# Even output residues from stored states: B at the even steps kept and topped up by accumulating DMAs on GpSimd's queue, in place of K0 and a decayed B

## The chip, the cores and the metric

The kernel runs on one core of one Trainium2 chip. The metric is the device time of one execution in microseconds (us). Five engines work side by side, each on its own instruction queue in order: TensorE (PE, matrix products into PSUM), VectorE (DVE), ScalarE (ACT), GpSimd (POOL) and SyncE (SP, which here only issues DMAs). They meet at semaphores.

## The reference

One input x (2048 steps of 512 channels) goes through two branches, and a gate mixes them.

```python
def _A_ref(x, Lambda_re, Lambda_im, B_re, B_im, C_re, C_im, log_dt, Dskip):
    Lam_bar = jnp.exp(dt * Lam)                     # 512 complex decays
    B_bar = ((Lam_bar - 1.0) / Lam)[:, None] * Bmat
    Bu = jnp.einsum("bld,pd->blp", x + 0j, B_bar)
    for t in range(L):
        h = Lam_bar[None, :] * h + Bu[:, t, :]
        hs.append(h)
    y = 2.0 * jnp.einsum("blp,dp->bld", hseq, Cmat).real + x * Dskip[None, None, :]
...
def _B_ref(x, wqkv, w_phi, wo):                     # 32 heads of 16: linear attention
    phi_q = concat[softmax(pq), softmax(-pq)]; phi_k = the same of pk
    o = phi_q (phi_k^T v) / (phi_q . sum phi_k + 1e-6)
    return o.reshape(B, S, D) @ wo
...
g = _sigmoid((x * gate_w).sum(-1, keepdims=True))
return g * a + (1 - g) * b
```

## The kernel before

The time axis is cut by residue: step t = 8c + r belongs to cell c (256 of them) and residue r (0 to 7), so x lies in SBUF as xT with the 16 tiles ordered by residue (tile ti = 2r + a holds residue r and cells of half a). The 512 complex states are four blocks j of 128 (PT = 4). The factor (Lam_bar - 1)/Lam is folded into C, so that states are driven by plain B.

Branch A, per block j:

- `st_l(j)` scales B by Lam_bar (two scalings of 128x1024 and two VectorE adds) and transposes the result by DMA into LBT: a B that is one step decayed.
- `st_g(j, dst, ri)` forms the drive of two residues at once on PE: four products with BT at residues 1 and 5 (dst 0) or 3 and 7 (dst 1), four with LBT at the even residues just before them, then for dst 1 products with diagonal matrices `dg` (powers of Lam_bar) that carry the drive on to residue 7. The results are copied from PSUM to `uv`.
- `st_z(j)` scans over the 256 cells on VectorE and gives the state at residue 7, in H3; `st_h4(j)` adds residue 3 to H3, and `st_h(j)` makes residues 1 and 5 in H1. So only the odd residues have states.
- `st_c(j)` makes C2, which is C times the folded factor: two scalings of 128x1024 and two VectorE adds. `st_r(j)` makes a second one, WKV[:, 0:2], which is C2 times Lam_bar, for the even residues (their state is the decayed odd state before them). `st_K(dtile)` makes K0T = B times C2 plus the skip on the diagonal, 8 products of 128x512 and one of 128x128 and a copy, four times: the direct effect of the input of an even step on its own output.
- `st_y(n)` (n = 0 to 15, tiles in the order of residues 7, 3, 5, 1, 0, 4, 2, 6) forms the output of a tile: eight products with the states; then four with x: 128x128 ones with the diagonal Dd at odd residues, 128x512 ones with K0T at even residues.

Branch B: `st_k`, `st_v`, `st_q` are the projections (matrix products and copies to SBUF), `feat_max`, `feat_min`, `feat_exp`, `feat_sum` the two softmaxes, `st_a` gathers phi_k^T v. `feat_sum` ends with a DMA transpose of the features of q (phT). `st_o(n)` forms a tile of attention, `st_O` transposes it by DMA (oT), `st_t(n)` adds its product with Wo onto the PSUM bank of `st_y(n)` and scales it by the gate, `st_R` stores it.

The order of everything is written out by hand: ORDER is a list of steps, each token running its step (a Python generator) up to its next `yield`. Each engine takes its instructions in that order. `@` gives the step its PSUM banks, and `:D` puts a copy or a scaling on VectorE in place of ScalarE. GpSimd makes the table of decays near the start (`st_M`) and then has nothing to do. SP issues every DMA but five small ones.

Of the kernel before, what the change touches and what calls it, by code (L numbers as in the profile page):

```python
# [20 lines left out]
P = 128  # L21
# [3 lines left out]
Z@0 Z Z Z Z Z Z B B B B Lk W00@1 W01@2 W00:D W01:D Lk W10@3 W10 W11@4 W11:D Lx T0@1 T0 f1@5 f0@2 f1:D Lx Lx f0 Z f2@6  # L25
V@7 V f2:D f3@4 P T3@0 T1@1 T2@5 f3 k0@2 T3 P P P2 P2 k0 U P2 P2 Lx Lx Lx U P2 Ln U k3@4 P4 U Lv T1 P4 k0 P4 P3 P2 Ln
i1 i3 V2@1 i1 k1@0 k1 k5@2 k1 P3 M V2 Lq i3 i1 gw i1 i1 i3 i3 x0 i3 k4@3 n0 T2 x0 i0 Lq k11@0 k10@6 k5 x0 n0 k3 i0 i2
k10 x0 Lb k4 n0 k2@5 Lb k2 i2 i0 i0 i0 i2 i2 i2 v1@4 k7@6 k7 v1 n0 x0 n0 l0:D L k11 x1 n1 k9@5 k6@1 l1:D l1:D Lx x1
v0@6 n1 x1 n1 l0:D x1 n1 w3@4 l0 l0 l1 l1 l0 x1 n1 l3:D e0 k6 k9 e0 v2@7 v2 v0 x2 n2 s0 w0@3 D w0 x2 v5@0 v5 e1 s0 x2
k8@2 g000@1 n2 x2 l1 k8 s0 n2 s0 s0 g001@5 g001 g001 n2 g000 g000 w2@0 e1 D x2 n2 k13@3 Lx g011@2 s0 l2 k13 x3 s1 s0  # L30
l3 w1@5 w1 Lb s1 Lc g011 g010@1 Lb l3 Lc g011 g011 g010 g010 g010 x3 s1 c0 g100@3 g010 g011 a0@56 x3 g010 g011 a0 z0
e2 x3 z0 n3 s1 k15@7 n3 g111@2 c0 z0 z0 z0 z0 k15 c1:D g101@1 g100 g101 l2 w3 n3 k14@7 z0 c1 g100 g101 l2 c0 k12@4 w2
n3 z0 x3 c1 n3 k14 s1 g110@3 g110 k12 l2 x4 z0 e2 e2 l2 z0 n4 x4 g110 g110 g111 g111 g111 v6@4 h0 H0 l3 x4 g111 g110
g201@7 v4@0 c0 g110 g111 v3@1 n4 H0 z1 z1 q1@2 x4 H0 s1 s1 v6 g200@4 h0 g200 e2 H0 H0 z1 z1 q1 v3 n4 e3 e3 e3 a1 a1 s2
q0@1 q0 z1 s2 z1 q3@2 q3 n4 s2 z1 z1 g200 v4 s2 z1 x4 n4 s2 z1 e3 q2@3 s3 q2 N0 s3 g201 g201 X0 q4@2 q4 s3 X0 h0 h0
g211@4 N0 H1 X0 s2 g211 g211 v7@7 Lc g211 q6@2 q6 e4 q5@3 H1 H1 X0 g210@0 g210 l3 g210 q5 v10@1 v7 g210 e4 g211 g211
s2 s2 g210 g210 s3 N0 s3 h0 h1 z2 z2 v10 s3 N0 Lc h0 a2 a2 z2 e4 z2 a2 a2 e4 c1 H1 X0 N0 H1 q10@4 q7@7 q7 N1 q10 h0 X1
q8@1 q8 g300@0 N1 X1 g301@3 g301 s4 c2 z2 E0 g300 E0 N1 g311@1 g300 s4 z2 g301 s4 X1 E0 g310@4 z2 g311 N1 h1 g311 E0
z2 v11@0 v11 g311 s3 g310 g310 q12@7 g310 g311 c3 X1 g310 s4 s4 z2 g310 z2 v8@0 S0 g311 v14@3 z3 z3 H2 s4 H2 v8 h1 S0
v14 H2 S0 q15@4 z3 v12@1 v12 z3 S0 S0 q12 a3 q11@0 z3 z3 q15 v9@3 v13@1 S0 S0 q13@4 v9 q9@7 q11 z3 H2 H2 v15@0 z3 s3  # L40
a3 h1 h1 h2 s4 s4 a3 a3 a4 q14@3 v13 a4 h1 h1 q9 v15 c3 c3 z3 z3 c3 c2 h2 c2 c2 Lo S0 h2 H3 h2 h2 a4 a4 G H3 H3 h2 G
h2 G H3 H3 y2@7 S0 S0 h3 q14 y1@0 h3 X1 N1 h3 h3 K3@1 G K3 N2 X2 Y Y Y K2@2 K2 y2 Y y1 y1 q13 E1 E1 E1 y2 h3 S0 X2 h3
E1 N2 K0@1 K0 h3 END o0@4 o0 o0 o2@2 S1 o2 K1@6 o0 o2 y7@1 y7 o2 K1 o3@4 r1 S1 o3 N2 S1 X2 N2 o1@2 o1 S1 o1 o1 y3@6 o3
O0 o3 O1 r1 y3 y3 X2 S1 y7 S1 y5@2 y5 y6@3 X2 S1 N2 r0 S1 r0 r0 S1 S1 y0@4 y0 t1 E2 E2 N3 r0 S1 r1 E2 y0 E2 t2 t2 X3
t3 t3 t0 r1 r2:D r2:D t0 S2 y6 X3 R1 t1 o4@6 o4 r2 N3 S2 o5@4 X3 o4 N3 o5 o5 X3 y6 y5 o4 y4@0 y4 o5 y4 o6@6 S2 r3 r3
r2 S2 o6 o6 r3 y9@4 r3 y11@5 y9 y11 S2 S2 o6 S2 o7@6 O2 R0 o7 o7 t4 S2 t5 N3 X3 N3 t4 o7 S2 E3 S2 E3 y9 E3 y11 y14@0
O3 o8@6 t5:D y13@2 o8 o8 y14 S2 t6 o8 E3 S3 R2 o9@6 S3 S3 S3 t7 t6 o9 o9 o9 y8@3 y8 t7 o10@6 S3 S3 S3 S3 y13 o10 y13
y12@1 o10 o10 O4 S3 o11@6 o11 o11 o11 y8 t8 S3 t9 t8:D t9:D S3 y12 o12@6 o12 y12 O5 o12 o12 y10@4 o13@6 o13 o13 o13 R4
y10 y10 O6 o14@6 o14 o14 o14 O7 y14 t10 t10:D o15@6 o15 t11 R3 o15 o15 O8 t11:D y15@34 R5 t12 t13 t12 t13:D R6 t14
t14:D R7 y15 y15 t15 t15:D t15 t15:D R8 R8  # L50
# [16 lines left out]
def kernel(  # L67
# [32 lines left out]
    ZP = 2  # L100
# [63 lines left out]
    K0T = const.tile([P, KT, D], BF16, name="K0T")  # L164
# [14 lines left out]
    dg = pBC.tile([P, 6, PT, P], BF16, name="dg")  # L179
    DG_NMI, DG_MR, DG_MI, DG_NNI, DG_NR, DG_NI = range(6)  # L180
    (S_LR, S_LI, S_NMI, S_MR, S_MI, S_NNI, S_NR, S_NI, S_NBI, S_BR) = range(10)
    par = pBC.tile([P, 21, PT], F32, name="ssm_par")
    dgs = pBC.tile([P, 10, PT], F32, name="dgs")
    dgv = pBC.tile([P, 6, PT, 4], BF16, name="dgv")
    Bn = pBC.tile([P, PT, 2, D], BF16, name="Bn")
    CT = pBC.tile([P, PT, 2, D], BF16, name="CT")
    ft_g = tc.tile_pool(name="feat", bufs=1, reuse_waits="tile")
# [7 lines left out]
    LBT = pAC.tile([P, 2, KT, Pst], BF16, name="LBT")  # L195
# [175 lines left out]
    def st_M():  # L371
# [16 lines left out]
        mn3 = dgs[:, S_NMI:S_NMI + 6, :].rearrange("p (a b) j -> p b a j", b=3)  # L388
# [6 lines left out]
    def st_D():  # L395
        nc.vector.tensor_copy(out=dgv[:].rearrange("p k j f -> p (k j) f"),
                              in_=dgs[:, S_NMI:S_NMI + 6].rearrange("p k j -> p (k j)").unsqueeze(2).to_broadcast([P, 6 * PT, 4]))
        yield
        VT(out=dg[:].rearrange("p k j (c f) -> p (k j) c f", f=4),
           in0=ident[:].rearrange("p (c f) -> p c f", f=4).unsqueeze(1).to_broadcast([P, 6 * PT, 32, 4]),  # L400
           in1=dgv[:].rearrange("p k j f -> p (k j) f").unsqueeze(2).to_broadcast([P, 6 * PT, 32, 4]), op=ALU.mult)
        yield
# [6 lines left out]

    def st_l(j):  # L410
        lr, li = uv[j][:, 0], uv[j][:, 1]
        scaled(lr, Bn[:, j], dgs[:, S_LR, j:j + 1])
        yield
        scaled(li, Bn[:, j], dgs[:, S_LI, j:j + 1])
        yield
        VT(out=lr[:, 0], in0=lr[:, 0], in1=li[:, 1], op=ALU.subtract)
        yield
        VT(out=lr[:, 1], in0=lr[:, 1], in1=li[:, 0], op=ALU.add)
        yield
        trans(out=LBT[:, :, :, j * P:(j + 1) * P].rearrange("p r k s -> p (r k) s"), in_=lr.rearrange("p r d -> p (r d)"))  # L420
        yield
# [156 lines left out]

    def st_g(j, dst, ri):
# [4 lines left out]
        def cells(kt, r):  # L584
            return xT[:, kt, :].rearrange("p (r c) -> p r c", r=8)[:, r::4, :]

# [4 lines left out]
        for kt in range(KT):  # L591
            MM(out=pgq[:], lhsT=LBT[:, ri, kt, js], rhs=cells(kt, r1 - 1), start=False, stop=(dst == 0 and kt == KT - 1))  # L592
# [16 lines left out]

    def st_c(j):  # L610
        t = (Wo, K0T)[j % 2]
        a_, b_ = t[:, 0:2, :], t[:, 2:4, :]
        scaled(a_, CT[:, j], dgs[:, S_BR, j:j + 1])
        yield
        scaled(b_, CT[:, j], dgs[:, S_NBI, j:j + 1])
        yield
        VT(out=C2[:, 0, j], in0=a_[:, 0], in1=b_[:, 1], op=ALU.add)
        yield
        VT(out=C2[:, 1, j], in0=b_[:, 0], in1=a_[:, 1], op=ALU.subtract)
        yield  # L620

    def st_r(j):
        a_, b_ = CT[:, 2 * j % 4], CT[:, (2 * j + 1) % 4]
        scaled(a_, C2[:, :, j], dgs[:, S_LR, j:j + 1])
        yield
        scaled(b_, C2[:, :, j], dgs[:, S_LI, j:j + 1])
        yield
        VT(out=WKV[:, 0, j], in0=a_[:, 0], in1=b_[:, 1], op=ALU.add)
        yield
        VT(out=WKV[:, 1, j], in0=a_[:, 1], in1=b_[:, 0], op=ALU.subtract)  # L630
        yield
# [85 lines left out]
    def st_K(dtile):  # L717
        pk0 = bank([P, D], F32, "pk0")
        ds_ = slice(dtile * P, (dtile + 1) * P)
        for j in range(PT):  # L720
            MM(out=pk0[:], lhsT=Bn[:, j, 0, ds_], rhs=C2[:, 0, j], start=(j == 0), stop=False)  # L721
            MM(out=pk0[:], lhsT=Bn[:, j, 1, ds_], rhs=C2[:, 1, j], start=False, stop=False)  # L722
        MM(out=pk0[:, ds_], lhsT=ident[:], rhs=Dd[:, dtile, :], start=False, stop=True)
        yield
        evac(K0T[:, dtile, :], pk0[:])
        yield
# [14 lines left out]
    def st_y(n):  # L741
# [5 lines left out]
        src = H3 if r % 4 in (0, 3) else H1  # L747
        off = {7: ZP, 0: ZP - 1, 3: ZP + NC, 4: ZP + NC, 1: 0, 2: 0, 5: NC, 6: NC}[r] + a * P
        cw = WKV if r % 2 == 0 else C2
        for j in range(PT):  # L750
            for ri in range(2):
                for py, (c, w) in zip(pys, halves):
                    MM(out=py[:], lhsT=src[:, j, ri, off:off + P], rhs=cw[:, ri, j, c:c + w], start=(j == 0 and ri == 0), stop=False)  # L753
            if j % 2:
                yield
        for kt in range(KT):
            xs = xT[:, kt, ti * P:(ti + 1) * P]
            if r % 2 == 0:
                for py, (c, w) in zip(pys, halves):
                    MM(out=py[:], lhsT=xs, rhs=K0T[:, kt, c:c + w], start=False, stop=False)  # L760
            else:
                MM(out=pys[0][:, kt * P:(kt + 1) * P], lhsT=xs, rhs=Dd[:, kt, :], start=False, stop=False)
# [122 lines left out]
```

## Time and profile before

| | |
|---|---|
| median of 3 runs | 158.71 us (158.57 to 159.26) |
| the profiled execution, its own time | 159.32 us |
| span of that execution, first to last instruction | 157.6 us |
| granted TensorE clock | 1.000 |
| PE busy | 150.5 us, 95% of the span, 1054 matmuls |
| DVE busy | 137.0 us, 87% |
| ACT busy | 126.4 us, 80% |
| POOL busy | 9.3 us, 6% |

The span is shorter than the execution's own time by 1.72 us that lie around it, and the median of the runs is 0.61 us under the profiled execution. "Busy" is the time in which an instruction of the engine was in flight; matmuls overlap each other, so the time that one keeps PE from the next is read from the starts of a run of them, not from its duration. In the lists of groups, the duration of one instruction stands after the busy time, and after the bar the idle time of the engine in front of the group.

### The profile page before, as it was taken

The page shows a single profiled execution, that of the slowest core. Times are in us where ns is not written, and L with a number is a line of the kernel's source. Part 1 is how long each engine was busy: PE and PEld are TensorE (multiplying, and loading weights), DVE is VectorE, ACT ScalarE, POOL GpSimd, SP SyncE. Part 2 cuts the span into 40 slices and gives each one's busy share as a digit, 9 for nine tenths or more (in the row PEclk, how much of TensorE's full clock was granted, in tenths as well). Part 3 has the DMA queues.
Part 4 walks back from the last instruction along what each step waited for, and adds up shares of the span by engine and source line. Part 5 has one row for each costly group of instructions (what it writes and reads, how often), then busy time and mean ns, then how long its engine had stood idle before and what let it go on. Part 6 is the DMA issues. An engine that isn't in the chain of part 4 may idle for free.

```text
span 157.6 us, 2913 instructions
## 1 busy us (share of the span) xinstructions
PE 150.5 (95%) x1054; PEld 77.5 (49%) x1054; DVE 137.0 (87%) x330; ACT 126.4 (80%) x233; POOL 9.3 (6%) x29
## 2 busy tenths in 40 slices
PE   6799799999999999999999999999999999999991
PEld 2554343545444544654444654555455444545570
DVE  4799699999999999999999999989999959553732
ACT  3499899799999999999999999997998496212110
POOL 6007800000000000000000000000000000000000
PEclk9999999999999999999999999999999999999999
DMA  5999989970029200000000019602793996795761
GB/s 133 175 213 280 241 176 205 202 119 4 0 45 178 44 0 6 0 0 0 4 0 0 0 19 264 121 2 49 138 213 95 148 212 154 136 208 128 165 201 33
DMA packets 52407, 16.99 MB, mean 108 GB/s; under 512 B 47145, under 2 KB 52393, under 8 KB 52393
## 3 DMA queue, kind: packets, MB, share of 16 engines
q1 hardware_dynamic: 51776, 16.78, 52.1%
q8 instruction: 8, 0.13, 0.4%
q10 hardware_dynamic: 552, 0.02, 0.2%
q14 instruction: 7, 0.05, 0.1%
q0 software_dynamic: 64, 0.00, 0.0%
HBM read 3.17 MB, written 2.10 MB: 33 GB/s over the span
## 4 chain that ended last, share of the span: by engine, by line
PE 58%; ACT 23%; DMA 8%; SPq 5%; DVE 3%; issue 1%; DVEq 0%
PE PS L753 18%; PE PS L466 9%; PE PS L808 9%; ACT EE L527 6%; PE PS L760 4%; SPq L216 4%; DMA Bn<-in_A_B_im_dram 4%; PE PS L592 3%; ACT Xq L125 3%; ACT uv L125 3%; PE PS L773 3%; PE PS L722 2%; PE PS L721 2%; PE PS L589 2%; DMA LBT<-uv 2%; PE PS L571 2%
## 5 line engine op out<-in xcount | busy, mean ns | idle before, releaser
L527 ACT ACTIVATE EE<-EE 128x1024 bf16<-128x1024 bf16 x32 | 34.6, 1179 | 0.0
L466 PE MATMUL PS<-WKV,xT 128*128 128x512 bf16 x128 | 30.4, 379 | 0.8 <-DMA WKV<-in_B_wqkv_dram 0.8
L466 PEld LDWEIGHTS <-xT 128*128 128x128 bf16 x192 | 18.1, 98 | 21.2 <-DMA WKV<-in_B_wqkv_dram 1.3
L125 ACT CAST Xq<-PS 128x512 bf16<-128x512 f32 x32 | 20.7, 708 | 0.7 <-PE PS L466 0.5
L753 PEld LDWEIGHTS <-H 128*128 128x128 bf16 x136 | 12.8, 98 | 12.9
L786 DVE TENSOR_TENSOR on<-PS,rd 128x512 bf16<-128x512 f32 x16 | 10.7, 687 | 6.9 <-ACT rd L780 6.9
L592 PE MATMUL PS<-xT,LBT 128*128 128x512 bf16 x64 | 15.9, 379 | 0.1
L589 PE MATMUL PS<-xT,BT 128*128 128x512 bf16 x64 | 15.8, 379 | 0.0
L753 PE MATMUL PS<-WKV,H 128*128 128x512 bf16 (+1 forms) x72 | 15.6, 355 | 0.0
L808 PE MATMUL PS<-Wo,oT 128*128 128x512 bf16 (+1 forms) x68 | 15.4, 366 | 0.0
L466 PE MATMUL PS<-Wq,xT 128*128 128x512 bf16 x64 | 15.4, 379 | 0.0
L753 PE MATMUL PS<-C,H 128*128 128x512 bf16 x64 | 14.9, 379 | 0.0
L777 ACT ACTIVATE ld<-PS 128x32 f32<-128x32 f32 x16 | 3.4, 214 | 11.7 <-PE PS L773 11.6
L125 ACT CAST vx<-PS 128x512 bf16<-128x512 f32 x16 | 11.9, 775 | 0.0
L125 ACT CAST uv<-PS 128x256 bf16<-128x256 f32 (+1 forms) x24 | 11.4, 573 | 0.0
L504 DVE TENSOR_TENSOR sm<-EE 128x2048 bf16<-128x2048 bf16 (+1 forms) x9 | 9.9, 1100 | 0.8 <-ACT EE L527 0.8
L592 PEld LDWEIGHTS <-LBT 128*128 128x128 bf16 x64 | 6.1, 98 | 7.7 <-DMA LBT<-uv 0.6
L589 PEld LDWEIGHTS <-BT 128*128 128x128 bf16 x64 | 6.3, 98 | 7.3 <-DMA xT<-in_A_x_dram 0.2
L521 DVE TENSOR_TENSOR EE<-mn,Xq 128x2048 bf16<-128x2048 bf16 (+1 forms) x9 | 9.9, 1097 | 0.0
L515 DVE TENSOR_TENSOR EE<-Xq,mx 128x2048 bf16<-128x2048 bf16 (+1 forms) x9 | 9.9, 1097 | 0.0
L814 DVE TENSOR_SCALAR ot<-PS,G 128x512 bf16<-128x512 f32 (+1 forms) x9 | 6.2, 690 | 4.1 <-PE PS L808 3.9
L542 DVE TENSOR_TENSOR EE<-EE,rc 128x2048 bf16<-128x2048 bf16 x8 | 9.6, 1217 | 0.0
(169 smaller groups left out, 289.7 us busy)
## 6 DMA issues: line engine op xcount, KB each, us to landing
out_dram<-ot SPq DMA_DIRECT2D x7, 256.0 KB, 2.3
C<-in_B_wqkv_dram SPq DMA_DIRECT2D x2, 256.0 KB, 3.1
C<-in_A_x_dram SPq DMA_DIRECT2D x2, 256.0 KB, 5.0
Bn<-in_A_B_re_dram SPq DMA_DIRECT2D x1, 512.0 KB
WKV<-in_B_wqkv_dram SPq DMA_DIRECT2D x1, 512.0 KB
Bn<-in_A_B_im_dram SPq DMA_DIRECT2D x1, 512.0 KB, 6.4
Wo<-in_B_wo_dram SPq DMA_DIRECT2D x1, 512.0 KB
oT<-on SPq DMA_TRANSPOSE x9, 3.2
```

The lines of the kernel that those rows point to most:

```text
L125: nc.scalar.copy(out=out_ap, in_=in_ap)
L466: MM(out=pt[:], lhsT=xT[:, kt, ti * P:(ti + 1) * P], rhs=W[:, kt, :], start=(kt == 0), stop=(kt == KT - 1))
L504: VT(out=dst, in0=cur[:, :, :, 0:n, :], in1=cur[:, :, :, n:2 * n, :], op=op)
L515: VT(out=half(EE, 0), in0=X5, in1=live["mx", p].to_broadcast([P, L, 8, Dh, 4]), op=ALU.subtract)
L521: VT(out=half(live["EE", p], 1), in0=live["mn", p].to_broadcast([P, L, 8, Dh, 4]), in1=X5, op=ALU.subtract)
L527: aexp(out=EE[:, l_], in_=EE[:, l_], func=ACT.Exp)
L542: VT(out=E5[:, u:u + 2], in0=E5[:, u:u + 2], in1=rc[:, u:u + 2].to_broadcast([P, 2, 2 * NB, Dh, 4]), op=ALU.mult)
L589: MM(out=pgq[:], lhsT=BT[:, ri, kt, js], rhs=cells(kt, r1), start=(kt == 0), stop=False)
L592: MM(out=pgq[:], lhsT=LBT[:, ri, kt, js], rhs=cells(kt, r1 - 1), start=False, stop=(dst == 0 and kt == KT - 1))
L753: MM(out=py[:], lhsT=src[:, j, ri, off:off + P], rhs=cw[:, ri, j, c:c + w], start=(j == 0 and ri == 0), stop=False)
L786: VT(out=live["on", g_][:, u], in0=pn[:, :, :, 0:Dh], in1=rd[:].unsqueeze(3).to_broadcast([P, 2, 16, Dh]), op=ALU.mult)
L808: MM(out=py[:], lhsT=oT[:, g, :], rhs=Wo[:, g, h * w:(h + 1) * w], start=False, stop=(g == HG - 1))
```

## The change

Three things change, and ORDER is new.

1. The even residues get states of their own. `st_b(j, pr, ri)` (new) forms B x at two even residues (pr 0: residues 0 and 4, pr 1: 2 and 6), four products of 128x512 and a copy to `eb`. `st_g` takes the decayed drive from `eb` by two products with new diagonals of Lam_bar (dg grows from 6 to 9 of them), where it had four with LBT; `st_l` and LBT go. `st_p(j, pr)` (new) then adds Lam_bar times the odd state before it to `eb`: it scales the states into the buffers t1 and t2, and two DMAs on GpSimd's queue add these to `eb` in place.
2. `st_c` scales into C2 directly, and a DMA on GpSimd's queue adds the second term; its two VectorE adds go.
3. With states at all residues, `st_y` uses C2 throughout and Dd at every residue. `st_r`, `st_K` and K0T go.

`eb` lies in the place of K0T and, for the blocks 2 and 3, in that of Bn. t1 is CT[:, j], and t2 lies in dg. The core of the diff:

```diff
 ORDER = """
-Z@0 Z Z Z Z Z Z B B B B Lk W00@1 W01@2 W00:D W01:D Lk W10@3 W10 W11@4 W11:D Lx T0@1 T0 f1@5 f0@2 f1:D Lx Lx f0 Z f2@6
...
+Z@0 Z Z Lk Lk B Z Z Z Z W00@1 Lx Lx B W01@2 B B W01:D W10@3 T0@4 W11@5 W00:D T1@6 f1@2 T0:D Lv W10 Lx T2@1 V@3 T1:D V
...
+S2 S2 N3 y5@2 p21 y5 S1 y5 o6@0 N3 o7@6 p31:D R0 y4@3 y4 y4 p01 O2 t4 S2 o7 o6 X3 t5 o7 p01 N3 p31:D o6 o6 y9@0 o7 p11
+S2 p21 y9 S2 E3 E3 R1 E3 E3 t4:D O3 o8@6 S2 t5:D y9 y8@1 o8 y8 S3 S3 S3 t6 p21 o8 o8 p01 o9@2 o9 o9 S3 o9 t7 O4 S3
+y11@6 S3 S3 S3 y8 y10@7 t6 t7 o10@2 y10 o10 o10 o11@4 S3 S3 y11 y11 y10 t8 t9 p31 o10 o11 o11 o11 t8:D S3 t9 y14@4
...
+    eb = [eb01[:, 0], eb01[:, 1], Bn[:, 0:2], Bn[:, 2:4]]
...
-        VT(out=dg[:].rearrange("p k j (c f) -> p (k j) c f", f=4),
...
+        for k in range(3):
+            VT(out=dg[:, 3 * k:3 * k + 3].rearrange("p k j (c f) -> p (k j) c f", f=4),
...
-    def st_l(j):
...
+    def st_b(j, pr, ri):
+        pb = bank([P, N2], F32, "pb")
+        for kt in range(KT):
+            MM(out=pb[:], lhsT=BT[:, ri, kt, j * P:(j + 1) * P], rhs=cells(kt, 2 * pr), start=(kt == 0), stop=(kt == KT - 1))
+        yield
+        evac(eb[j][:, ri, pr, :], pb[:])
+        yield
...
-        for kt in range(KT):
-            MM(out=pgq[:], lhsT=LBT[:, ri, kt, js], rhs=cells(kt, r1 - 1), start=False, stop=(dst == 0 and kt == KT - 1))
+        da, db = ((DG_LR, DG_NLI), (DG_LI, DG_LR))[ri]
+        MM(out=pgq[:], lhsT=dg[:, da, j, :], rhs=eb[j][:, 0, dst], start=False, stop=False)
+        MM(out=pgq[:], lhsT=dg[:, db, j, :], rhs=eb[j][:, 1, dst], start=False, stop=(dst == 0))
...
+    def add_by_dma(out_ap, in_ap):
+        nc.gpsimd.dma_start(out=out_ap, in_=in_ap, accum_op=ALU.add)
...
     def st_c(j):
...
+        scaled(C2[:, 1, j], CT[:, j, 0], dgs[:, S_BR, j:j + 1])
+        yield
+        scaled(C2[:, 0, j], CT[:, j, 1], dgs[:, S_NBR, j:j + 1])
+        yield
+        scaled(CT[:, j], CT[:, j], dgs[:, S_NBI, j:j + 1])
+        yield
+        add_by_dma(C2[:, :, j], CT[:, j])
         yield
...
-    def st_K(dtile):
...
+    def st_p(j, pr):
+        E_ = eb[j][:, :, pr]
+        t1 = CT[:, j]
+        t2 = dg[:].rearrange("p k j s -> p (k j s)")[:, 2 * N2 * j:2 * N2 * (j + 1)].rearrange("p (a c) -> p a c", a=2)
+        cuts = ((0, NC, H3, ZP - 1), (NC, N2, H3, ZP + NC)) if pr == 0 else ((0, N2, H1, 0),)
+        for c0, c1, src, z0 in cuts:
+            scaled(t1[:, :, c0:c1], src[:, j, :, z0:z0 + c1 - c0], dgs[:, S_LR, j:j + 1])
+            yield
+        add_by_dma(E_, t1)
+        yield
+        for ri in range(2):
+            for c0, c1, src, z0 in cuts:
+                scaled(t2[:, ri, c0:c1], src[:, j, 1 - ri, z0:z0 + c1 - c0], dgs[:, (S_NLI, S_LI)[ri], j:j + 1])
+                yield
+        add_by_dma(E_, t2)
         yield
...
-        cw = WKV if r % 2 == 0 else C2
+        if r % 2:
+            src = H3 if r % 4 == 3 else H1
+            off = {7: ZP, 3: ZP + NC, 1: 0, 5: NC}[r] + a * P
+            hs = [[src[:, j, ri, off:off + P] for ri in range(2)] for j in range(PT)]
+        else:
+            off = r // 4 * NC + a * P
+            hs = [[eb[j][:, ri, r % 4 // 2, off:off + P] for ri in range(2)] for j in range(PT)]
...
-            if r % 2 == 0:
-                for py, (c, w) in zip(pys, halves):
-                    MM(out=py[:], lhsT=xs, rhs=K0T[:, kt, c:c + w], start=False, stop=False)
-            else:
-                MM(out=pys[0][:, kt * P:(kt + 1) * P], lhsT=xs, rhs=Dd[:, kt, :], start=False, stop=False)
+            h, c = (0, kt * P) if len(pys) == 1 else (kt // 2, kt % 2 * P)
+            MM(out=pys[h][:, c:c + P], lhsT=xs, rhs=Dd[:, kt, :], start=False, stop=False)
```

The names pXY that the prediction uses are ORDER's: p21 is `st_p(2, 1)`, block 2 and residues 2 and 6.

## The prediction

> **What bounds the kernel now.** I read the page's busy tenths first, then the chain of waits, then the windows by stage, and last the groups by shape.
>
> ```profile
> PE   6799799999999999999999999999999999999991
> ACT  3499899799999999999999999997998496212110
> DMA  5999989970029200000000019602793996795761
> PE 58%; ACT 23%; DMA 8%; SPq 5%; DVE 3%; issue 1%; DVEq 0%
> ```
>
> PE is full from slice 8 to slice 39; ACT is nearly as full up to slice 32, then has room. The stages say the same (columns: length, then busy time of PE, PEld, DVE, ACT, POOL, clock, DMA share, GB/s):
>
> ```profile
> 60.00:92.00 32.00, 31.81 (x270) 16.85 (x269) 31.97 (x71) 32.00 (x59) 0.00 (x0) 1.00 0.01 2
> 92.00:120.00 28.00, 28.00 (x207) 14.67 (x205) 27.49 (x62) 27.08 (x49) 0.00 (x0) 1.00 0.58 123
> 120.00:140.00 20.00, 19.97 (x138) 9.93 (x136) 15.47 (x27) 11.02 (x24) 0.00 (x0) 1.00 0.81 154
> ```
>
> Three engines are full at once from 60 to 92 us, GpSimd does nothing there, and the DMA engines rest until 92. Which of the three sets the pace is told by adding up issue intervals. The chain of waits shows PE's (start, length, what):
>
> ```profile
> 99.39 0.45 PE PS L762 x8
> 126.12 1.73 PE PS L760 x8
> 152.35 0.87 PE PS L760 x8
> 153.70 0.92 DVE ot L814 x2
> ```
>
> Eight 128x512 products in 1.73 us are 0.216 each, eight 128x256 in 0.87 are 0.109, eight 128x128 in 0.45 are 0.056. With 0.032 for 128x68 (L773) and 0.025 for one column, the kernel's products are 584 x 0.216 + 48 x 0.109 + 100 x 0.056 + 256 x 0.032 + 64 x 0.025 = 146.9 us. The time at which PE reaches a product, less the product work ahead of it, is 4.2 us at 8 us, 5.6 at 24, 6.3 at 48, 6.7 from 72 to 96, 7.0 at the end. So PE lost its time before 24 us and then 1.4 us in 130: it sets the end, and 3.9 us of scaling and storing follow its last product (153.7 to 157.6). ACT's instructions add up to 123.2 us plus a table load of 1.3, DVE's to 134.4.
>
> **What PE gains.** All of it is on the path, if the others keep up. K0T's forming goes (L721, L722: 32 products of 512 columns and 4 of 128): -32 x 0.216 - 4 x 0.056 = -7.1 us. At even residues Dd takes the place of K0T: 28 of 512 and 8 of 256 go, 32 of 128 come: -6.0 - 0.9 + 1.8 = -5.1. The drive of the even step by `eb` and the new diagonals adds 32 of 512: +6.9. `st_b`'s 64 products take the place of LBT's 64: 0. Net **-5.4 us** (rounded once; 141.5 left).
>
> **ACT** goes up. Gone: 16 scalings of 1024 columns at 1.05, 4 K0T copies at 0.47, 11 scalings of 512 moved to DVE at 0.61, 3 xT copies at 0.48: 26.8 us. New: 5 scalings of 1024 for C2 at 1.05, 14 of 512 at 0.61, 12 of 256 at 0.40 (between the 0.26 of a copy of that size and the 0.61 of 512), 16 copies of `eb` at 0.47, 3 outputs at 0.59, 3 casts at 0.47: 29.3. Net +2.5, giving 125.8. Token by token along the new ORDER, ACT's sum runs at most 0.8 us ahead of PE's (1.2 in the old one), because what is added falls where PE has `st_b`: I put it at 0. If that fails, up to 2.5 is the price.
>
> **DVE** goes down: 24 adds of 512 at 0.335, 8 scalings of 1024 at 0.395, 3 outputs at 0.75, 2 WKV casts at 0.64 and one Xq at 0.33 (15.1 us) go. Three dg instructions for one (+0.9), 3 xT copies (1.0), 3 scalings of 1024 (1.2), 21 of 512 at 0.23 and 4 of 256 at 0.15 (both estimates from the 1024 row, 5.4) come: 8.5. Net -6.6. DVE isn't the bound, so 0.
>
> **The start.** Two things move. The LBT transposes leave SP (`LBT<-uv`, 3.37 us in the chain at 23.06): PE is late for them by about 0.3 only. But the second Wq transpose (H) moves behind two BT and one CT:
>
> ```profile
> 12.45 5.69 SPq L231 DMA_TRANSPOSE H<-in_B_wqkv_dram  x2
> 18.36 3.27 SPq L226 DMA_TRANSPOSE BT<-Bn  x2
> ```
>
> BT can't start before Bn_im lands at 17 to 18.4; then 3.27 for BT, 1.33 for CT and 2.85 for H end the issue at 24.5 to 25.8, and it lands 1.5 to 3 later, at 26 to 28.8. PE wants it at product work 20.2, about 25.8 us: there stands w3, the first piece of the folding of Wq (`fold`), which reads all of it. So 0 to 3 us of stall, and every product queued behind w3 waits with it: I take **+1.0**, from the early half, since a BT for one block of the two needs only part of the 3.27. A gain of 0.8 is possible on the other side: PE's wait for WKV at 16 us (0.84) goes because Wv (Lv) is now needed later.
>
> **The adding DMAs.** Twenty of them (4 for C2, 16 for `eb`), 256 KB each in 256 runs of 1 KB, all through GpSimd's queue. Nothing like them is in the trace. Nearest rows:
>
> ```profile
> L255 POOL DMA_DIRECT2D vec_m<-in_A_Dskip_dram x1 | 0.8, 766 | 0.0
> out_dram<-ot SPq DMA_DIRECT2D x7, 256.0 KB, 2.3
> oT<-on SPq DMA_TRANSPOSE x9, 3.2
> phT<-EE SPq DMA_TRANSPOSE x8, 4.5
> ```
>
> GpSimd's own issue took 0.77 us for 1 KB; a plain 256 KB store lands in 2.3 us, a transpose of the same size in 3.2, of 512 KB in 4.5. An addition reads two operands and writes one, so I take 3 to 4 us from issue to landing (bounds 2.3 and 4.5), and 1.0 us of issue (bounds 0.5, SP's issue of such a store, and 2.85, half of the row of H above, the longest issue of one transpose). Bandwidth is there: a store occupies all 16 DMA engines for about 0.75 us, and 0.01 of the DMA time is used from 60 to 92 us.
>
> What matters is when the sums must be there. In the new ORDER the first even tile (y9) starts at product work 115, about 122.5 us; it reads blocks 2 and 3 of residues 0 and 4 (`eb` in Bn). y14 comes at 134.5 us, y12, which wants p21 and p31, at about 137. The first addition (p01) can be issued at about 84 us, the last (the second of p31) at about 124; p20's second at about 109, 13 us ahead of y9. At 3 to 4 us each, side by side, every sum is early and the cost is 0.
>
> The other cost is in the engines' own order. The two additions to one `eb` are ordered, and t1 and t2 are reused: p10's t1 waits until c1 has landed, p21's until p20's first, p31's until p30's first, p21's t2 until p20's second. ACT waits in its own order: behind such a wait stand branch B's ld, rd and the exponentials, for which `st_o` and so PE wait. By product work the tightest is p31's t1, 1 to 2 us after p30's landing at 3.5 us each; p21's has 4. With landings 1 us longer, ACT waits 0 to 1 us, and it is already near PE. I take **+0.8** for this together with GpSimd's and DVE's meetings (next part); bounds 0 and 4.
>
> **A row and a rule on GpSimd beside DVE.** While DVE ran two 128x1024 instructions between 15.77 and 17.05 us, a GpSimd instruction on 128x16 took far longer than one of the same shape before it:
>
> ```profile
> 13.31 0.21 POOL L375 TENSOR_TENSOR ssm_par<-dgs 128x16 f32<-128x16 f32 x1
> 15.88 1.24 POOL L382 TENSOR_TENSOR ssm_par<-dgs,vec 128x16 f32<-128x16 f32 x1
> 15.77 0.68 DVE L515 TENSOR_TENSOR EE<-Xq,mx 128x1024 bf16<-128x1024 bf16 x1
> 16.37 0.68 DVE L521 TENSOR_TENSOR EE<-mn,Xq 128x1024 bf16<-128x1024 bf16 x1
> ```
>
> GpSimd gave way for the length of what DVE had running: 1.24 against 0.21, ending when DVE did. An issue of 1.0 us may thus become 2, which still leaves 2.7 us on average between additions (85 to 125 us, 15 of them) unfilled. The Trainium skill ("SBUF — State Buffer", section "Who interferes with whom") goes further and speaks against this change: the descriptors of a DMA on GpSimd's queue are written through a port pair that it shares with DVE, one holds it for the whole of an instruction, and the other stands still; two-input VectorE instructions block only GpSimd's reads. The row fits the last part; no run so far shows an issue held. By the skill's "DMA: Bandwidth & Descriptors" (section "Anatomy of one DMA — SWDGE (gpsimd) path") such a transfer takes 2.0 us plus bytes at 436 GB/s, an estimate of 2.6 us for 256 KB, with which my 0.8 would be about 0.3.
>
> **Sum.** 157.6 - 5.4 + 1.0 + 0.8 = 154.0 us of span; plus 1.72 around it 155.7 for a profiled execution; less 0.61 for the median: **155.1 us**. The measurement can tell about 0.5% from no change, so "the same" is 157.9 to 159.5.
>
> **Rivals.**
>
> *R1, the queue works one addition after another, slower.* If an addition holds the queue from its issue to its landing, T each, the fifteen from p01's first (85 us) to p31's last end at 85 + 15T. y12 wants that by 137: up to T = 3.5 us nothing happens. At T = 4.0 they end at 145 and PE stands still 8 us: 155.1 + 8 = 163. At 4.5 it is 15 more: 170. For it: 3.2 to 4.5 us for transposes of such sizes, and the fixed order of adds on one tile. Against: plain stores of 256 KB land in 2.3, and SP's transposes overlap. 0.18.
>
> *R2, DVE is held by GpSimd's issues.* About 19 scalings of DVE fall between p01 and p31. If an issue of 1.0 us shuts out DVE, an issue is under way 16 x 1.0 / 45 = 36% of that time, a DVE instruction waits half an issue on average: 19 x 0.36 x 0.5 = 3.4 us; at 1.5 us, 7.6. DVE is 98% busy at 92 to 120 us, and PE waits for its copies: 158 to 162, 160 the middle. The row above shows the opposite direction only. The shut-out for a whole instruction is also the rule of the Trainium skill's "SBUF — State Buffer" named above, and as yet no row bears it out in this direction. 0.10.
>
> *R3, the start costs more.* H lands at 28.8, 3.0 after w3's turn, and PE has nothing else in its order: 2.0 more than I took, and 0.4 for Wq's copies trailing on ACT: 157.5. 0.10.
>
> *R4, ACT is the bound.* Its +2.5 us falls where ACT is 100% busy (60 to 92), PE's gain is used up by waits for copies, and the end stays about 158.7. Against it: after 120 us ACT is only 55% busy. 0.04.
>
> **How the numbers follow.** Forecast 0.58 (154 to 156.5). R1, R2 above: nearly all slower, with some of R2 in "the same". R3 mostly faster, R4 the same. Faster: 0.58 less 0.03 for costs that take the gain, plus 0.06 of R3 = 0.61. Same: 0.03 + 0.04 of R3 + 0.04 of R4 + 0.02 of R2 = 0.13. Slower: 0.18 of R1 + 0.08 of R2 = 0.26. The range: the low end has no stall at the start, the gain of 0.8 there, and about a third of the 0.8 for landings and meetings unspent (155.1 - 1.0 - 0.8 - 0.3 = 153.0); at the top it takes in R3, R4, R2 and the first of R1, **153.0 to 163.0**, leaving out R1's long half (0.1) and about 0.07 below or between.
>
> **What will show it.** Right: PE's product work near 141.5 us, its lag still about 7 to 8 at y9, no idle PE before y9 and y12; additions landing in 3 to 4 us; GpSimd's issues about 1 us. The first wrong sign for R1: additions landing at equal steps of over 3.5 us, and PE's wait before y9, y14 or y12 ended by a DMA to `eb`. For R2: DVE scalings of 512 columns well above 0.3 us where they lie beside an issue. For R3: a PE wait at w3 ended by the DMA into H. The forecast is wrong if the median is over 157.9.

## The result, and the profile after

The changed kernel takes 168.06 us (median of 4 runs, 165.26 to 168.69) against 158.99 of the kernel before in the same job. The ratio, here and below taken over the undisturbed runs of both alone (here 165.26 and 167.5), is 1.0463 (95% interval 1.0327 to 1.0598): slower, where 155.1 us was forecast. The profiled execution is the one of 165.26 us, its span 163.6. It is the fastest of the four; what the others lose beyond it, 2.2 to 3.4 us, no trace shows.

The page of the kernel after: busy tenths in 40 slices of 4.1 us, DMA queues, and the shares of the chain.

```profile
PE   6899879999999999999999999999389977699990
PEclk9999999999999999999999999999957999999998
DMA  5999999974000004290009999799997699999251
q0 software_dynamic: 5504, 5.25, 24.5%
DVE 27%; ACT 26%; PE 20%; DMA 15%; SPq 7%; issue 2%; DVEq 0%; ACTq 0%
```

PE is full up to slice 27 as before, then has holes (a 3 in slice 28, 7 and 6 in 32 to 34), and for two slices the granted clock falls (5 and 7). The DMA row, which had zeros from slice 14 to 22 and gaps after that, is full from slice 21 on. In the chain PE's share fell from 58% to 20%, DMA's rose from 8% to 15%. Queue 0 is GpSimd's: its twenty additions held 24.5% of the time of 16 engines, 24.5% x 163.6 / 20 = 2.0 us of all sixteen for each (the times of its packets added up; where packets of several transfers are under way at once, each has its own time counted).

Windows of the kernel after (length, busy PE, PEld, DVE, ACT, POOL, clock, DMA share, GB/s; a share over 1: packets of several transfers under way at once):

```profile
60.00:92.00 32.00, 31.54 (x198) 15.43 (x200) 31.99 (x79) 32.00 (x63) 8.57 (x8) 1.00 0.44 60
92.00:120.00 28.00, 24.21 (x217) 13.26 (x219) 27.03 (x64) 25.04 (x52) 10.82 (x9) 0.97 1.18 162
120.00:140.00 20.00, 17.71 (x108) 8.33 (x109) 11.71 (x18) 11.25 (x23) 3.67 (x3) 0.88 1.02 164
```

From 60 to 92 us nothing is wrong. From 92 to 140 us the DMA share went from 0.58 and 0.81 to 1.18 and 1.02, and PE lost time. What it waited for, in the list of waits (engine, line, releaser: total us, times, longest):

```profile
PEld L805 <- DMA oT<-on: 5.2, 2, 2.9
PE PS L805 <- DMA oT<-on: 4.6, 2, 2.8
PE PS L770 <- DMA phT<-EE: 1.8, 2, 1.3
PE PS L457 <- DMA xT<-in_A_x_dram: 1.6, 1, 1.6
```

Not one of them is a sum in `eb`. They are the transposes of branch B, whose own work the change leaves as it was, and an x tile at the start. In the kernel before, the same list has no wait for an oT or a phT. The lists of ScalarE and VectorE after the change have no wait for an addition either. The chain of waits shows the two worst, and the timelines GpSimd's last three additions and SP's issue of the phT behind them (start, length):

```profile
113.71 5.31 DMA oT<-on
119.07 2.74 PE PS L805 x6
130.42 10.63 DMA phT<-EE
141.09 0.43 PE PS L770 x8
```

```profile
128.65 1.20 POOL L611 DMA_DIRECT2D Bn<-dg  x1 [11.22 <-ACT dg L410]
129.38 1.71 POOL L611 DMA_DIRECT2D eb<-dg  x1
130.10 2.21 POOL L611 DMA_DIRECT2D Bn<-dg  x1
130.42 7.82 SPq L549 DMA_TRANSPOSE phT<-EE  x1
```

A phT of 512 KB that landed in 4.5 us before takes 10.63 when three additions are issued just ahead of it: 6.1 us more, and three times 2.0 is 6.0. Most of it is the issue, which holds SP's queue for 7.82 us, against 1.3 to 3.5 for a phT in the kernel before. After the wait for oT, six products take 2.74 us where eight took 1.73: the clock.

PE's arrival less the product work ahead of it (the measure of the prediction) is 6.5 us from 28 to 56 us, 7.7 at 92, 8.1 from 104 to 114; then 11.5 at 119, 14.6 at 126, 16.5 at 136, 18.0 from 141 to the end. 141.5 + 18.0 + 4.1 of tail = 163.6. So the kernel is on the forecast's course up to 114 us (forecast for the end: 8.6) and loses 9.9 us in the next 27.

### The profile page after: what moved, and what is told of

The parts are those of the page before. It is cut to its first block, busy times and chain, and to the rows that moved or that the text cites. A ratio compares the mean times of both kernels' runs of the same rounds, so it can differ in the third digit from the quotient of the medians.

```text
span 163.6 us, 2923 instructions
## 1 busy us (share of the span) xinstructions
PE 148.0 (90%) x1028; PEld 76.5 (47%) x1046; DVE 132.1 (81%) x325; ACT 128.0 (78%) x252; POOL 33.5 (20%) x50
## 3 DMA queue, kind: packets, MB, share of 16 engines
q0 software_dynamic: 5504, 5.25, 24.5%
## 4 chain that ended last, share of the span: by engine, by line
DVE 27%; ACT 26%; PE 20%; DMA 15%; SPq 7%; issue 2%; DVEq 0%; ACTq 0%
ACT EE L518 8%; PE PS L753 7%; DMA phT<-EE 6%; PE PS L805 6%; SPq L218 5%; DMA xT<-in_A_x_dram 4%; PE PS L457 3%; DMA oT<-on 3%; ACT Xq L127 3%; DVE EE L533 3%; DVE sm L495 3%; ACT uv L127 3%; DVE mn L495 2%; DMA Wc<-in_B_w_phi_dram 2%; DVE mx L495 2%
## 5 line engine op out<-in xcount | busy, mean ns | idle before, releaser
L805 PE MATMUL PS<-Wo,oT 128*128 128x512 bf16 (+1 forms) x65 | 16.7, 393 | 4.9 <-DMA oT<-on 4.6
L588 PE MATMUL PS<-xT,BT 128*128 128x512 bf16 x64 | 16.1, 379 | 0.1
L753 PE MATMUL PS<-C,H 128*128 128x512 bf16 x64 | 16.0, 402 | 0.0
L576 PE MATMUL PS<-xT,BT 128*128 128x512 bf16 x64 | 15.6, 379 | 0.1
L809 ACT ACTIVATE ot<-PS,G 128x512 bf16<-128x512 f32 x11 | 7.3, 684 | 10.3 <-PE PS L805 10.3
L127 ACT CAST uv<-PS 128x256 bf16<-128x256 f32 (+1 forms) x24 | 13.1, 633 | 0.0
L611 POOL DMA_DIRECT2D eb<-CT x4 | 4.8, 1324 | 38.0 <-ACT CT L410 37.8
L805 PEld LDWEIGHTS <-oT 128*128 128x128 bf16 x68 | 6.5, 103 | 11.0 <-DMA oT<-on 5.2
L410 ACT ACTIVATE dg<-H,dgs 128x256 bf16<-128x256 bf16 (+1 forms) x18 | 10.8, 675 | 0.0
L127 ACT CAST vx<-PS 128x512 bf16<-128x512 f32 x16 | 10.6, 788 | 0.0
L753 PEld LDWEIGHTS <-H 128*128 128x128 bf16 x64 | 6.5, 104 | 8.1 <-issue 2.2
```

The lines of the kernel that those rows point to most:

```text
L127: nc.scalar.copy(out=out_ap, in_=in_ap)
L410: nc.scalar.mul(out=out_ap, in_=in_ap, mul=s_)
L576: MM(out=pb[:], lhsT=BT[:, ri, kt, j * P:(j + 1) * P], rhs=cells(kt, 2 * pr), start=(kt == 0), stop=(kt == KT - 1))
L588: MM(out=pgq[:], lhsT=BT[:, ri, kt, js], rhs=cells(kt, r1), start=(kt == 0), stop=False)
L753: MM(out=py[:], lhsT=hs[j][ri], rhs=C2[:, 1 - ri, j, c:c + w], start=(j == 0 and ri == 0), stop=False)
L805: MM(out=py[:], lhsT=oT[:, g, :], rhs=Wo[:, g, h * w:(h + 1) * w], start=False, stop=(g == HG - 1))
```

## The experiments

Theory D: the additions fill the DMA engines and delay the transposes on SP's queue. Rival Q: issuing on GpSimd, or waiting for additions, holds VectorE or ScalarE. Rival S: the new order puts the transposes too late by itself. The time of the kernel before beside them was 159.5 to 159.6 us.

### e1: the same DMAs with few bytes

```diff
-        add_by_dma(E_, t1)
+        add_by_dma(E_[:, :, 0:32], t1[:, :, 0:32])
-        add_by_dma(E_, t2)
+        add_by_dma(E_[:, :, 0:32], t2[:, :, 0:32])
```

> The 16 additions to eb carry 64 bytes of each 1 KB run, so 15/16 of what they should add is left out; the number of DMAs, their runs, issues, waits and places in every queue stay. Theory D (the additions fill the DMA engines: 24.5% of 163.6 us for 20 of them is 2.0 us of all 16 engines each, and the transposes oT and phT on SP's queue wait behind them): oT lands in about 3.2 us and phT in about 4.5 again, PE's waits before t2, t6 and o10 go, and with them the half clock after the first: 165 to 168 less about 9 us, 155.5 to 158. Rival Q (issuing on GpSimd, and DVE or ACT held by it or by the waits on the additions): unchanged, 165 to 169. Rival S (the new order puts the transposes too late by itself): unchanged as well.

157.39 us (157.0 to 157.65), 0.9892 of the kernel before (0.9858 to 0.9926). From its page and list of waits:

```profile
PEclk9999999999999999999999999999999999999999
q0 software_dynamic: 5504, 1.31, 9.5%
PE PS L805 <- DMA oT<-on: 1.3, 2, 0.7
```

As many packets as ever (5504), a quarter of the bytes, and 8.3 us gone from the span of the profiled execution (163.6 to 155.3); the two long waits and the drop of the clock with them. Order, issues and queue are those of the kernel after, so S falls, and the issues of Q are worth little. The other half of Q, waiting for additions, is eased here too, since they land sooner (those from CT to `eb` in 2.8 us instead of 5.0); that it isn't the cause rests on the lists of waits above and on e9.

### e2: the six late additions on VectorE

```diff
-        add_by_dma(E_, t2)
+        if (j, pr) in ((2, 0), (3, 0), (1, 1), (2, 1), (0, 1), (3, 1)):
+            VT(out=E_, in0=E_, in1=t2, op=ALU.add)
+        else:
+            add_by_dma(E_, t2)
```

> The six second additions that are issued last (p20, p30, p11, p21, p01, p31) are VectorE adds of 128x1024 at 0.60 us instead of DMAs. Theory D: 12 us of DMA time less after 108 us; PE's waits before t6 and o10 (1.8 + 1.3 us) go and the one before t2 shrinks, since only one or two additions are left near it: 157 to 161. VectorE is full until 112 us, which costs up to 1.2 us. Rivals Q and S: 165 or more.

157.99 us (157.62 to 158.13), 0.9921 (0.9889 to 0.9952): the whole computation, and already faster than the kernel before. Six 0.6 us adds take the place of 12 us of all DMA engines. Five of them run after 118 us, and from 120 to 140 us VectorE is busy for 16.5 of 20 us.

### e6 and e7: which three of the six

```diff
 e6:  if (j, pr) in ((2, 0), (3, 0), (1, 1)):   # issued at 108, 111, 116 us
 e7:  if (j, pr) in ((2, 1), (0, 1), (3, 1)):   # issued at 128.6 to 130.1 us
```

> The changed kernel with the second additions of p20, p30 and p11 (issued at 108, 111 and 116 us) as VectorE adds. Theory D: the wait before t2 (2.8 us) and the half clock after it (about 3 us lost) go, the waits before t6 and o10 (3.3 us) stay: 160 to 163.5. If the half clock doesn't hang on that wait: 163.5 to 166.

> The complement: the second additions of p21, p01 and p31 (issued at 128.6 to 130.1 us) as VectorE adds. Theory D: phT of the last group lands in 4 to 5 us instead of 10.6, the waits before t6 and o10 (3.3 us) go, those before t2 stay with the half clock: 163 to 165.5. Rivals Q and S: 165 to 169 in both of these runs.

162.05 us (159.38 to 162.51; 1.0073, 1.0013 to 1.0133) and 161.13 (159.97 to 162.93; 1.0088, 1.0055 to 1.0121). The first as expected in amount, but the wait that was left took another place; the second below its range. The list of waits of e6, then of e7:

```profile
PE PS L808 <- DMA oT<-on: 4.3, 2, 3.9
```

```profile
PE PS L808 <- DMA oT<-on: 2.2, 1, 2.2
PE PS L773 <- DMA phT<-EE: 0.6, 1, 0.6
```

With PE earlier in e6, the last three additions met an oT (issued at 124.04, landed 7.50 later) instead of the phT, and the clock fell to 0.59 from 132 to 136 us. So each group of three can delay whatever transpose stands behind it; the two losses don't add up to single waits that could be named ahead.

### e3: the additions by GpSimd itself

```diff
-        add_by_dma(E_, t1)
+        nc.gpsimd.tensor_tensor(out=E_, in0=E_, in1=t1, op=ALU.add)
-        add_by_dma(E_, t2)
+        nc.gpsimd.tensor_tensor(out=E_, in0=E_, in1=t2, op=ALU.add)
```

> The 16 additions to eb are GpSimd's own additions of 128x1024 instead of DMAs on its queue. Theory D: nothing of eb passes through the DMA engines, so the transposes land as before, 156 to 158, if GpSimd needs under 2.5 us each (15 of them between 85 and 124 us). Rival Q in the form of a meeting of GpSimd and VectorE: VectorE's instructions beside GpSimd's get longer, and the time stays above 160 although no transpose waits. Rival S: 165 or more.

181.94 us (181.27 to 185.42), 1.1415 (1.1365 to 1.1464). The DMA share from 84 to 124 us is 0.16, and still this is the slowest kernel of all. Rows of its groups and its timeline:

```profile
L715 POOL TENSOR_TENSOR eb<-eb,CT 128x1024 bf16<-128x1024 bf16 x4 | 15.6, 3899 | 40.8 <-ACT CT L410 39.6
91.21 2.21 DVE L412 TENSOR_SCALAR m<-H,dgs 128x512 bf16<-128x512 bf16 x1
99.26 2.61 DVE L681 TENSOR_TENSOR m<-m,uv 128x1024 bf16<-128x1024 bf16 x1
```

In the kernel after these VectorE rows take 0.35 and 0.68 us. VectorE's busy time rose from 132.1 to 159.2 us, and PE's largest waits in total are for VectorE (6.3 and 5.4 us). Beside GpSimd's own additions some VectorE instructions take about as long as an addition (2.4 to 2.5 us there); others keep their time (0.42 for one of 128x512 at 89.73 us), and then it is the additions that are long (two in 9.09 us). That is the meeting that R2 feared, but from GpSimd's arithmetic. Beside its DMA issues, in the kernel after, such a scaling takes what it takes alone (the first row):

```profile
53.64 0.35 DVE L412 TENSOR_SCALAR mc<-H,dgs 128x512 bf16<-128x512 bf16 x1
91.90 1.20 POOL L611 DMA_DIRECT2D Bn<-CT  x1 [4.18 <-DVE m L681]
92.98 0.34 DVE L412 TENSOR_SCALAR mc<-H,dgs 128x512 bf16<-128x512 bf16 x1
93.30 1.20 POOL L611 DMA_DIRECT2D eb<-dg  x1 [0.20 <-issue]
93.51 0.34 DVE L412 TENSOR_SCALAR m<-H,dgs 128x512 bf16<-128x512 bf16 x1
```

Of the six scalings of 512 columns that overlap an issue there, five took 0.34 us and one (at 35.51) 0.50.

### e9, after a flawed e5: the additions alone, on the kernel before

```diff
         aexp(out=rd[:], in_=ld[:], func=ACT.Exp, scale=-1.0, bias=nge[:, ti:ti + 1])
+        for d_ in {0: (dgt[:, 1],), 2: (dgt[:, 2],), 3: (Bn[:, 0],), 4: (Bn[:, 1],), ...}.get(n, ()):
+            nc.gpsimd.tensor_copy(out=after_rd[:], in_=rd[:].rearrange("p a b -> p (a b)"))
+            nc.gpsimd.dma_start(out=d_, in_=dgt[:, 0], accum_op=ALU.add)
```

> The kernel before, with ten adding DMAs of 256 KB on GpSimd's queue between buffers that nothing reads any more (CT, Bn), each released by the rd of a tile of st_o (104 to 130 us). Nothing of its order or work is changed, and no engine waits for them. Theory D (each fills all 16 DMA engines for 2.0 us): the DMA share of 0.58 and 0.81 from 92 to 140 us is 32 us of 48, with 20 more it is over 48, so transposes land 2 to 5 us later and PE waits: 161 to 168. Rival S (the changed order is at fault): 159. Rival Q (issues of 1.2 us hold VectorE): VectorE's instructions beside an issue get longer, ten times up to 1 us, little of it on the path after 120 us: 159 to 161.

> The experiment of ten adding DMAs on the kernel before, mended: there the buffers of CT were still used by st_r, and ScalarE waited 5.9 and 3.5 us for two of the additions. Now nine of them, between dg and Bn, whose last readers have run by 104 us, released by rd of st_o as there. Theory D: 18 us of all 16 DMA engines between 104 and 131 us, beside the 32 that are in use from 92 to 140: phT and oT land later where they meet (up to 6 us for three together), and PE waits for them, 2 to 6 us with any half clock: 161 to 166. Rival S (the changed order alone delays the transposes): 159 to 160.

e5 took 173.85 us (173.01 to 175.16), outside its range, but CT was still read in it, against what its expectation says: a scaling of ScalarE waited 5.9 us for an addition, so it tells little.

e9 has the fault mended: 165.12 us (164.3 to 166.46), 1.0353 (1.0297 to 1.041). From its list of waits and its chain:

```profile
PE PS L813 <- DMA oT<-on: 3.1, 3, 1.5
PE PS L774 <- DMA phT<-EE: 2.3, 1, 2.3
124.71 9.30 DMA phT<-EE
```

(`dgt` is `dg` cut in three.) Old order, old arithmetic, and nine additions that no engine waits for (and nine GpSimd copies of 128x32 that time their issues): 5.6 us lost, at oT and phT again. This is theory D by itself.

### e10: the same DMAs as plain copies

```diff
-        add_by_dma(E_, t1)
+        nc.gpsimd.dma_start(out=E_, in_=t1)
-        add_by_dma(E_, t2)
+        nc.gpsimd.dma_start(out=E_, in_=t2)
```

> The changed kernel with the 16 DMAs to eb as plain copies, same queue, same 256 runs of 1 KB, nothing added (the even states are overwritten instead of summed up). If it is the adding that takes 2.0 us of the 16 DMA engines, and a copy takes the 0.75 of SP's stores, this falls to 156.5 to 159. If it is the queue or its kind of descriptors, whatever they do, it stays at 164 to 169.

158.46 us (156.94 to 162.93), 0.9905 (0.9864 to 0.9945); the even states are overwritten here, not summed up. From its page and its DMA issues, and in the last line from the page of e9:

```profile
q0 software_dynamic: 2432, 5.25, 13.3%
C<-CT POOLq DMA_DIRECT2D x4, 256.0 KB, 4.5
eb<-CT POOLq DMA_DIRECT2D x4, 256.0 KB, 2.8
q0 software_dynamic: 1360, 2.36, 8.6%
```

The bytes are those of the kernel after (5.25 MB). The queue's time is 13.3% of 155.9 = 20.7 us instead of 40.1. In e3, where C2's four are the only additions, queue 0 has 3.8% of 180.4 = 6.9 us, 1.7 for each; less these, a copy costs (20.7 - 6.9) / 16 = 0.87 us, near the store's 0.75. So it isn't the queue. Nor are the packets the same: 64 of queue 0's belong to small loads, so an addition has (5504 - 64) / 20 = 272, and a copy (2432 - 64 - 4 x 272) / 16 = 80. But e9's additions, with (1360 - 64) / 9 = 144 packets each, still held 8.6% x 164.8 / 9 = 1.6 us. Most of the difference is thus put down to the adding; a copy in 272 packets wasn't run.

### e8: PE kept busy in the wait

```diff
+        if n == 5:
+            for _ in range(28):
+                MM(out=pn2[:, 1, 272:512], lhsT=ph[:, 7, :], rhs=Wo[:, 0, 0:240], start=False, stop=True, skip_group_check=True)
```

> The changed kernel with 28 products of 240 columns (2.9 us at 0.103, an estimate from 0.109 for 256) of no use behind st_o(5), into columns of its bank that nothing reads, so that PE is busy while it waits for oT before t2. If the half clock from 118 to 125 us comes from that idle stretch, it goes and the time falls by about 3 us, to 162.5 to 165.5, though PE has more to do; if not, 165 to 169.

164.55 us (162.94 to 165.4), 1.0283 (1.0192 to 1.0374). The profiled execution is 2.4 us shorter than that of the kernel after (161.2 and 163.6), though PE has 2.9 us more to do; the intervals of the two ratios overlap, so the times alone don't tell the kernels apart. The clock does, in the same window of the two, first of the kernel after:

```profile
120.00:124.00 4.00, 3.78 (x10) 1.41 (x10) 0.38 (x1) 1.99 (x4) 0.00 (x0) 0.50 1.12 241
```

```profile
120.00:124.00 4.00, 3.87 (x36) 2.05 (x35) 3.97 (x9) 3.23 (x8) 0.00 (x0) 1.00 1.15 185
```

Ten products of 512 columns at clock 0.50 are 2.2 us of product work; the 36 at 1.00, twenty of them small, are 4.2. In the kernel after, PE's lag rises from 11.5 to 14.6 us between 119 and 126 us with a wait of only 0.2 in between. So about 3 of the 9.9 us that were lost after 114 us are a consequence of the idle stretch.

### e4 and e11: the start

```diff
 SP's order:  after  Ln Lq Ln Lx Lx    e4  Ln Lx Lx Lq Ln    e11  Ln Ln Lx Lx Lq (and e2's adds)
```

> Only SP's order at the start: the third and fourth pair of x tiles go ahead of the second half of B and of the first half of Wq. PE's wait of 1.6 to 2.1 us for an x tile at 19 to 21 us (it lands 6.2 us after its issue, behind 512 KB of B) should go, unless B's transposes, now 2.8 us later, make PE wait at the first st_b instead (about 26 us): a gain of 1 to 2 us, or 0. The waits after 112 us stay, 163 to 167.

> The six late additions on VectorE as in e2, and at the start the first half of Wq behind the second half of B and the third and fourth pair of x: the x tile that PE waits for (1.6 us at 20 us) is issued 1.2 us earlier and B too; the second half of Wq stays where it is. If the start is a matter of order: 0.5 to 1.3 us less than e2's 157.99, 156.6 to 157.6. If it is one of the bytes ahead of each transfer, the wait moves to Wq (w3) and nothing is won: 157.6 to 159.

e4: 169.76 us (169.24 to 170.03), none of the gain and above the expected 163 to 167. Its list of waits:

```profile
PE PS L417 <- DMA H<-in_B_wqkv_dram: 2.7, 1, 2.7
PE PS L576 <- DMA BT<-Bn: 1.4, 1, 1.4
```

The wait for x is gone, and Wq and B, pushed back, cost 4.1 us. e11 puts only half of Wq back: 157.20 us (157.09 to 157.43), 0.9852 (0.9818 to 0.9886), 0.8 below e2. PE now waits 0.3 us for x and 0.9 for Wq. This version beats both kernels.

### e12: C2's additions on VectorE too

```diff
-        add_by_dma(C2[:, :, j], CT[:, j])
+        VT(out=C2[:, :, j], in0=C2[:, :, j], in1=CT[:, j], op=ALU.add)
```

> As e2, and the four additions to C2 are VectorE adds of 128x1024 (0.60 us) as well, so the second part of the change is undone. Its DMAs run at 35 to 71 us, where the DMA engines have room: taking them away frees nothing. VectorE gets 2.4 us more where it is full. If VectorE sets the pace with PE there: 158.5 to 160.4; if it has slack: 157.6 to 158.4.

162.61 us (161.0 to 163.39), 4.6 above e2 and above its whole range. Its list of waits:

```profile
PE PS L588 <- ACT Bn L127: 3.2, 1, 3.2
ACT CT L410 <- DVE C L620: 3.0, 1, 3.0
```

VectorE's adds of 0.6 us came late in its full queue, ScalarE waited 3.0 us for one, and PE for ScalarE, with the clock down behind it (0.58 from 84 to 88 us). So in this order the change's second part pays where it stands: its DMAs run between 35 and 71 us, and from 40 to 55 us, for one, the share of the DMA engines in the kernel after is 0.00. How much of the 4.6 us an order made for VectorE's adds would save wasn't tried.

## Why the prediction was wrong, point by point

- **What bounds the kernel, and PE's -5.4 us**: right. Product by product PE follows the sum up to 114 us, and in e11, with the whole computation, what is left of the gain shows. (The prices shown add up to 146.8 us for PE, not 146.9, and ACT's 123.2 + 2.5 to 125.7; nothing hangs on either.)
- **ACT at 0, DVE at 0**: right. In the kernel after PE waits 0.2 us for a copy of ScalarE, and from 32 to 112 us PE is busy for 78.9 of 80 us, though ScalarE (80.0) and VectorE (79.9) are full beside it. VectorE's scalings of 512 follow each other in 0.26 us, where I had estimated 0.23. The +0.8 for waits on landings and meetings didn't show: neither engine waits for an addition.
- **The start, +1.0**: right in size by luck, wrong in place. PE's lag at 24 us is 6.5 against 5.6. But no wait was for H; it was for an x tile, issued behind Bn's second half, of which the prediction says nothing. e4 shows the stall that I had named, once H goes further back.
- **The adding DMAs: the step that failed.** "Bandwidth is there: a store occupies all 16 DMA engines for about 0.75 us" failed in both halves. The price was that of a store: an addition occupied 2.0 us, not 0.75 (1.7 with the engines nearly to itself). And the share of 0.01 that I set it against is the window of 60 to 92 us, while 12 of the additions were issued from 91.9 to 130.1 us, where the page I had quoted says 0.58 and 0.81. The sum that should have been made: 16.2 + 16.2 us in use from 92 to 140 us, plus 12 x 2.0 = 24, is 56 in 48. With 0.75 it is 41 in 48, which also leaves little. (In the kernel after, the two windows hold 1.18 x 28 + 1.02 x 20 = 53: overlapping packets can push a share above 1, so the sum is a warning and no hard limit.) What the step put at nothing cost 9.9 us of PE's time. I asked whether the sums would be there in time, and never who shares the sixteen engines with them.
- **Who waits**: I followed those who wait for a new DMA. Those that lost were old transfers on another queue, oT and phT, with no dependence on the change. Every sum in `eb` was in time; y9, y12 and y14 waited for none.
- **R1**: its time (163 to 170) came out by luck, its mechanism didn't. Additions landed in 4.4 us (C2's median) and in 4.9 to 8.8 later (medians of four), over the 3.5 that I had given as the limit. Yet three were issued within 1.5 us of each other and were under way at once, and no tile waited for one.
- **R2**: not at these issues. In e1 all twenty are there, and the time is below that of the kernel before; beside an issue five of six scalings took 0.34 us. The Trainium skill's "SBUF — State Buffer", section "Who interferes with whom", is borne out by e3, where GpSimd reads SBUF itself (0.35 us became 2.21). No run shows an issue that held VectorE for long; the most was that one 0.50 us.
- **R3, R4**: neither decided anything.
- **The landing, estimated at 2.6 us**: the estimate of 2.6 us after "DMA: Bandwidth & Descriptors" of the Trainium skill (section "Anatomy of one DMA — SWDGE (gpsimd) path") fits e10's plain copies from CT (2.7 and 2.8; those from dg took 3.7 and 4.7) and not the additions (4.4 for C2's, with the engines nearly free).

## What to carry to other kernels

Before work is moved onto DMAs, add up the DMA engines like any other engine: the time that all sixteen are held by what is there in that very window, plus the new transfers at their own price, against the length of the window. A queue of its own is no engine of its own: what loses is whatever stands behind the new transfers, here transposes that feed PE. The sum warns but doesn't decide. From 92 to 140 us the shares measured come to 0.79 x 28 + 1.04 x 20 = 42.9 us of 48 in e9, where PE waits 5.4 us for transposes, and to 1.03 x 28 + 0.90 x 20 = 46.8 in e2, where it waits 1.7. So look, too, at which transfers stand right behind each new one. The adding DMA was worth it where the engines rested (C2) and not where branch B's transposes run; six adds moved to VectorE, which has room there, turned 4.6% slower into 0.8% faster, and 1.5% with the start mended.

## What the runs showed of the hardware

- A DMA that adds 256 KB in SBUF in runs of 1 KB held all 16 engines for 1.7 us when nearly alone (e3) and 2.0 on average in the kernel after, against 0.87 for a copy on the same queue (e10, in fewer packets) and 0.75 for SP's store. It landed in 4.4 us when nearly alone, a copy in 2.7 to 4.7.
- An idle stretch of PE of 2.8 us, before t2 (`st_t(2)`, which waits for oT), was enough for the granted clock to fall to 0.50 from 120 to 124 us, and so was one of 2.2 us in e7 (0.75 there). 1.8 us before t6 was not, nor were waits of 2.4 and 2.6 us in e5, so the length alone doesn't settle it. With the stretch filled by useless products the clock stayed at 1.00. The Trainium skill's "TensorE: Matmul & The Clock Gate" (section "Part 1: The HAM clock gate") has the clock halved after one idle window of about 3.4 us; here 2.2 to 2.8 us could do it.
- GpSimd's addition of two 128x1024 tiles took 2.4 to 3.9 us (means of e3's four groups), and VectorE's instructions beside it up to six times their length (2.21 for 0.35).
